# Attention and adapters in one kernel: load tiles of 128 rows by 16 units in place of 256 rows by 8, two parts in place of four, ten adapter chains of four blocks, and a new order

## The chip, the cores and the metric

The kernel runs on one core of a Trainium2 chip. The metric is device time in microseconds (us) of one execution; the time before is the median of three runs. A profile is one further execution, taken by the hardware profiler; its span runs from the first to the last instruction of the core. Engines are named as in the profile: PE (TensorE, matrix multiply) and PEld (its weight loads), DVE (VectorE), ACT (ScalarE), POOL (GpSimd), SP (SyncE, which only issues DMAs). DMAs are issued from SP, ACT and POOL and carried out by 16 DMA engines.

## What is computed

Sliding-window attention (window 32 to both sides) over 8 batches of 8 heads, 576 positions, 64 numbers a head; then a mixture of adapters of rank 16, of which each token takes the best two of eight. Cut to what matters:

```python
batch, n_heads, seq, head_dim = (8, 8, 576, 64)      # q, k, v: float32
scores = scale * np.matmul(q, k.transpose(0, 1, 3, 2))
mask = np.abs(pos[:, None] - pos[None, :]) <= 32
scores = np.where(mask, scores, -1000000000.0)
attn = softmax(scores);  attn_out = np.matmul(attn, v)
x = attn_out.transpose(0, 2, 1, 3).reshape(4608, 512)  # all heads of a token side by side
logits = x @ w_gate                                    # 8 experts
w = softmax of the two largest logits
out = x + sum over the two of w * ((x @ A[e]) @ B[e])  # float32, 4608 x 512
```

## The kernel before

**Units and halves.** A unit is one head of one batch, 576 x 64 numbers. The 128 partitions are two halves of 64: batches 0 to 3 use the lower, batches 4 to 7 the upper (index `g` in the loads), so that one 128-row operation works on a unit of either half. Per half there are 32 units.

**Parts and tiles.** The work has four parts `s` (`SB = 4`), each one batch of either half, 8 units wide. q, k and v come in nine tiles `t`. Tiles `2s` and `2s+1` hold 256 rows of the 8 units of part `s`; query rows begin 32 later than key rows. Tile 8 (`XT`) holds the rest for all 32 units: keys 512 to 575, and for the queries rows 0 to 31 and 544 to 575.

**Loads.** `load_qk` (L305) brings each q or k tile with two DMAs of 512 KB from SP, one for each half, into a buffer `raw` (five of them, 1 MB each); the query tile 8 has four of 256 KB. Each partition gets 16 rows of one unit, 4 KB that lie together in memory; `run_parts` (L288) sets which: with `"h (n r) d -> n h (r d)"` the run of 16 rows, `n`, is the outer index and the head `h` the inner one. For tile 8 it is `"u (n r) d -> u n (r d)"`, the unit outside. A tile is cast to 16 bits in two halves (POOL, ACT or DVE), turned by PE into a PSUM bank (8 matmuls of 128 columns, L335, against `swap`, which also sorts the partitions by head, or `ident`), and copied out to `qT` or `kT` (L352). `load_v` (L371) issues four DMAs of 128 KB for each tile from POOL, which cast on the way; DVE turns them (L388).

**Attention.** `score(s, a)` takes key block `a` (64 keys) of all 8 heads of a part and of both halves: two matmuls put the mask down (L423), 16 multiply keys and queries (L429), ACT takes the exponential (L435). `pv` (L462) multiplies by v for five or six heads of a block `g` of 128 tokens (L475); DVE divides (L487, L494). Block `g` needs key blocks `2g-1` to `2g+1`. So block 0 needs tile 8's queries, and blocks 2 to 4 need the second tile of the part.

**Adapters.** `moe` (L503) is a chain for some blocks of both halves: transposes (L520), a copy out (L182 on ACT, L180 on DVE), the product with gate and A weights (L560), the choice of two experts in eleven small operations on DVE and one on ACT (L570 to L591), the gated product (L601), a transpose (L610), a copy out, the product with B (L634), the sum with x (by PE with a second matmul, L637, and a copy out, L645; or by DVE, L648), and a store of 128 tokens x 512 (SP, L655). Each part has two chains, of four and of six blocks: eight in all.

**Order.** Nothing is scheduled on the chip: the numbers of `ORDER` set the sequence in which all of these operations are handed to their engines, `ON` the engine where two could do it, `HOME` the buffer of a pool. Each engine works through its list strictly in turn. The DMAs that SP and ACT issue take eight semaphores (`DMAHW0` to `DMAHW7`) in turn, so a DMA waits until the eighth before it has landed.

Of the kernel before, what the change touches and what calls it, by code (L numbers as in the profile page):

```python
# [16 lines left out]
D = 64  # L17
NB = 9
NH = 8
SB = 4  # L20
XT = 2 * SB
GS = 172
# [81 lines left out]
def kernel(  # L104
# [14 lines left out]
    POOLS = {"B": 8, "raw": 5, "c16": 6, "v16": 3, "xq": 1,  # L119
             "qT": 2, "kT": 4, "vt": 4, "PT": 7, "xa": 2, "xb": 1, "xT": 1, "zs": 2, "zT": 2, "ob": 4,  # L120
# [4 lines left out]
    def many(name, shape, dt, pool=sb):  # L125
# [7 lines left out]
        "qT": many("qT", [128, NH, NB * 64], F16),  # L133
# [3 lines left out]
        "xa": many("xa", [128, 2, 2 * DD], F16),  # L137
        "xb": many("xb", [128, 2, 3 * DD], F16),
        "xT": many("xT", [128, 6, 4, 128], F16),
        "zs": many("zs", [128, 6, ER], F16),  # L140
        "zT": many("zT", [128, 6, 128], F16),
# [16 lines left out]
    swap = sb.tile([128, 128], F16, name="swap")  # L158
# [120 lines left out]
    grows = {w: x.rearrange("(g b) h n d -> g b h n d", g=2) for w, x in (("q", q), ("k", k), ("v", v))}  # L279
    qT, kT, vt = {}, {}, {}  # L280
    for s in range(SB):
        qT[s] = buf("qT", f"qT{s}")
    xq = buf("xq", "xq")

    def due_of(t):
        return {0: -100, XT: 24}.get(t, 72 * (t // 2) + 32 * (t % 2))

    def run_parts(w, t):  # L288

        r = []  # L290
        for g in range(2):
            x = grows[w][g]
            if t < XT:
                r0 = 256 * (t % 2) + (32 if w == "q" else 0)
                i = x[t // 2, :, r0:r0 + 256].rearrange("h (n r) d -> n h (r d)", r=16)
                r.append((g, 0, 128, i))
                continue
            u = x.rearrange("b h n d -> (b h) n d")
            rows = [(0, 512, 576)] if w == "k" else [(0, 0, 32), (64, 544, 576)]
            for p0, a, b in rows:  # L300
                i = u[:, a:b].rearrange("u (n r) d -> u n (r d)", r=16)
                r.append((g, p0, 2 * (b - a), i))
        return r

    def load_qk(w, t):  # L305
        due = due_of(t) + (32 if (w, t) == ("k", XT) else 0)
# [3 lines left out]
        dst = kT[t] if w == "k" else xq if t == XT else qT[t // 2]  # L310
# [7 lines left out]
        for hf in range(2):  # L318
# [37 lines left out]
    def ends(s):  # L356

        def go(eng):
            w = ap(qT[s]).bitcast(F32)
            o = dataclasses.replace(w, ap=[list(w.ap[0]), [272, 2], [288, NH], [1, 16]])  # L360
            i = ap(xq).bitcast(F32).rearrange("m (e u r) -> m e u r", e=2, r=16)[:, :, NH * s:NH * s + NH]
            (nc.scalar.copy if eng == "ACT" else nc.gpsimd.tensor_copy)(out=o, in_=i)  # L362
        op({"POOL": 0.45, "ACT": act(256)}, 0, go, bufs=[xq, qT[s]], need=[("qT", XT)], make=[("ends", s)],
           prio=due_of(2 * s) + (24 if s == 0 else -10))

    def load_v(t):
        v16, dst = buf("v16", f"v16_{t}"), buf("vt", f"vt{t}")
        vt[t] = dst
        due = 54 if t == XT else due_of(t) if t else -90
        for g in range(2):  # L370
            for f in range(2):  # L371
                p0 = 64 * g + 32 * f
                x = grows["v"][g]
                if t < XT:
                    r0 = 256 * (t % 2)
                    src = x[t // 2, :, r0:r0 + 256].rearrange("h (a f r) d -> f h a (r d)", f=2, r=32)[f]
                else:
                    src = x.rearrange("b h n d -> (b h) n d")[:, 512:576].rearrange(
                        "u (f r) d -> f u (r d)", f=2)[f]
# [15 lines left out]
    for s in range(SB):  # L395
        ends(s)
# [4 lines left out]
    def slot(u, a):  # L401

        s, h = divmod(u, NH)
        return (2 * s + a // 4, 4 * h + a % 4) if a < 8 else (XT, u)

    def score(s, a):

        ti = (s, a)
        ps = buf("B", f"ps{ti}", 2)
        PT[ti] = pt = buf("PT", f"PT{ti}")  # L410
        t = slot(NH * s, a)[0]
        need = {"mask", "ident", ("kT", t)}
        need |= {("qT", 2 * s)} if a < 5 else set()
        need |= {("qT", 2 * s + 1)} if a > 3 else set()
        need |= {("ends", s)} if a in (0, NB - 1) else set()
        lo, hi = max(0, 64 * a - 32), min(576, 64 * a + 96)
        c0 = lo - (64 * a - 32)

        def go():
            p = ap(ps).rearrange("m (i c) -> m i c", c=128)  # L420
            for j in range(2):
                m = slice(64 * j, 64 * j + 64)
                nc.tensor.matmul(out=p[:, 4 * j:4 * j + 4], lhsT=twice[m],  # L423
                                 rhs=bcast(mask[m], 1, 4), start=True, stop=False)
            for h in range(NH):
                sl = slot(NH * s + h, a)[1]
                for g in range(2):
                    m = slice(64 * g, 64 * g + 64)
                    nc.tensor.matmul(out=p[m, h, c0:c0 + hi - lo], lhsT=ap(kT[t])[m, 64 * sl:64 * sl + 64],  # L429
                                     rhs=ap(qT[s])[m, h, lo:hi], start=False, stop=h % 4 == 3)  # L430
        dur = mm(512) + 0.02 + 8 * (mm(hi - lo) + 0.004)
        pr = 72 * s + 8 * a
        op("PE", dur, go, bufs=[ps, kT[t], qT[s]], need=sorted(need, key=str),
           make=[("ps", ti)], prio=pr, mode=1, count=2 + 2 * NH)
# [5 lines left out]
    for s in range(SB):  # L440
        for a in range(NB):
            score(s, a)
# [3 lines left out]
    for s in range(SB):  # L446
        xs[s, 0], xs[s, 1] = buf("xa", f"xa{s}"), buf("xb", f"xb{s}")

    def x_part(s, g):

        return (xs[s, 0], g) if g < 2 else (xs[s, 1], g - 2)

    def pv(s, i0, n):

        items = [(NH * s + i % NH, i // NH) for i in range(i0, i0 + n)]
        token = (s, i0)
        po, rc = buf("B", f"po{token}", 2), buf("rc", f"rc{token}")
        xd, at = x_part(s, items[0][1])
        ops, bufs, need = [], {po}, set()
        for j, (u, g) in enumerate(items):  # L460
            mine = [(a, off) for a, off in ((2 * g - 1, 128), (2 * g, 64), (2 * g + 1, 0))
                    if 0 <= a < NB]  # L462
            for n, (a, off) in enumerate(mine):
                ti, pos = (s, a), u % NH
                t, sl = slot(u, a)
                ops.append((j, ti, pos, off, t, sl, n == 0, n == len(mine) - 1))
                bufs |= {PT[ti], vt[t]}
                need |= {("PT", ti), ("vt", t)}
        last = 9 * s + max(x[1][1] for x in ops)
# [11 lines left out]
        n = len(items)  # L481
# [20 lines left out]

    def moe(s, items, p0, step):  # L503

        xT = buf("xT", f"xT{s}{items[0]}")
        n = len(items)
        tok = (s, items[0])
        xd, first = x_part(s, items[0][1])

        def xp():  # L510

            return ap(xd).rearrange("p b (g c) -> p b g c", c=DD)[:, :, first:]
        for j in range(0, n, 2):
            two = items[j:j + 2]
            tp = buf("B", f"tx{s}{two}")

            def turn(two=two, tp=tp):
                for i, (b, g) in enumerate(two):
                    for c in range(4):
                        nc.tensor.matmul(  # L520
                            out=ap16(tp)[:, 512 * i + 128 * c:512 * i + 128 * c + 128],
                            lhsT=xp()[:, b, g - items[0][1]].rearrange("p (m c) -> p c m", c=4)[:, c],
# [3 lines left out]
               need=[("x", s, g) for _, g in two], make=[("tx", tok, j)], prio=pr, count=4 * len(two))  # L526
# [67 lines left out]
        for w, pz in enumerate(pzs):  # L594
# [25 lines left out]
            for j in range(0, k, 2):  # L620
                pair = [items[i] for i in mine[j:j + 2]]
                m = len(pair)
                pd, ob = buf("B", f"pd{s}{pair}", m), buf("ob", f"ob{s}{pair}")
                pq = pr2 + step * (0.4 + 0.2 * j)
                dt = (s, pair[0])

                def x_of(pair=pair, m=m):
                    return xp()[:, :, pair[0][1] - items[0][1]]
                by_pe = BY_PE(s, w, j)
# [28 lines left out]
    for s in range(SB):  # L658
        moe(s, [(b, g) for g in (0, 1) for b in range(2)], 72 * s + 46, 4)
# [105 lines left out]
```

## Time and profile before

| | |
|---|---|
| time, median of 3 runs | 165.09 us (164.57 to 165.52) |
| the profiled execution's own time, and its span | 166.1 us, 164.3 us |
| busy: PE, DVE, ACT, POOL | 118.9, 92.6, 81.8, 53.6 us |
| mean granted clock of TensorE | 0.873 of full speed |
| read from memory, written | 28.85 MB, 9.44 MB |
| loads of q and k | 34 DMAs of 512 KB and 4 of 256 KB, by SP: 18.87 MB |

The last line counts 18 DMAs for k, and 16 and 4 (of 256 KB) for q. A share is of the span unless it is called a share of the DMA engines: that is the mean over the 16 of them, and 1.00 or a little over it means that none was free. The GB/s beside it count the bytes as written, so that v, which arrives in 32 bits and is written in 16, counts half.

### The profile page before, as it was taken

To read this page: it belongs to the slowest core of one execution; us is meant where nothing else is said; L and a number is where in the kernel's file an instruction comes from. 1 tells how busy PE (TensorE), PEld (TensorE's weight loads), DVE (VectorE), ACT (ScalarE), POOL (GpSimd) and SP (SyncE) were. 2 spreads that over 40 slices of the span, in tenths; PEclk is the share of its full clock that TensorE was granted. 3 is DMA by queue.
4 is the path that set the end of the run, shared out by engine and by line. 5 is a ranking of instruction groups with operands and counts; after the bars stand their busy time and mean duration, and the time that the engine had idled before them with its cause. 6 is when DMAs were issued, how large, how long until landed. Compare 5 with 4: busy or idle time off the path is not lost.

```text
span 164.3 us, 5141 instructions
## 1 busy us (share of the span) xinstructions
PE 118.9 (72%) x2206; PEld 85.8 (52%) x2206; DVE 92.6 (56%) x187; ACT 81.8 (50%) x119; POOL 53.6 (33%) x90
## 2 busy tenths in 40 slices
PE   7804228627980695868989978998999999975740
PEld 3203215325850583658756757665768766765310
DVE  4003445106503554979789957776856768847720
ACT  4002006704392065767298645775688874833340
POOL 8962000054660729604736924208100000000000
PEclk9975555765696599999999999999999999999995
DMA  4999993999999999999999999991040046271285
GB/s 117 243 217 221 217 206 60 260 241 310 240 243 230 234 246 235 238 227 252 284 338 241 341 261 303 358 293 66 0 134 34 4 141 233 93 261 54 89 309 177
DMA packets 14566, 33.90 MB, mean 206 GB/s; under 512 B 4048, under 2 KB 4048, under 8 KB 14544
## 3 DMA queue, kind: packets, MB, share of 16 engines
q1 hardware_dynamic: 10464, 28.32, 61.3%
q0 software_dynamic: 2752, 4.72, 15.4%
q10 hardware_dynamic: 1328, 0.54, 1.9%
q8 instruction: 17, 0.28, 0.7%
q14 instruction: 5, 0.04, 0.1%
HBM read 28.85 MB, written 9.44 MB: 233 GB/s over the span
## 4 chain that ended last, share of the span: by engine, by line
PE 42%; DMA 37%; DVE 10%; issue 4%; ACT 2%; ACTq 1%; SPq 0%; POOL 0%; DVEq 0%; POOLq 0%
DMA raw<-in_q_dram 16%; DMA ob<-in_moe_A_dram 15%; PE banks L429 8%; PE banks L475 6%; DMA v<-in_v_dram 6%; PE banks L335 5%; PE banks L634 5%; PE banks L560 5%; PE banks L423 5%; PE banks L520 4%; PE banks L637 3%; DVE xb L494 3%; DVE xa L494 2%; PE banks L610 1%; ACT PT L435 1%
## 5 line engine op out<-in xcount | busy, mean ns | idle before, releaser
L327 POOL CAST c<-raw 128x1024 f16<-128x1024 f32 x28 | 28.5, 1049 | 51.6 <-DMA raw<-in_q_dram 36.3
L435 ACT ACTIVATE PT<-banks 128x1024 f16<-128x1024 f32 x36 | 36.0, 1028 | 18.5 <-PE banks L429 17.2
L335 PE MATMUL banks<-swap,c 128*128 128x128 f16 x256 | 21.2, 241 | 16.7 <-ACT c L325 6.8
L335 PEld LDWEIGHTS <-c 128*128 128x128 f16 x288 | 19.8, 110 | 23.9 <-ACT c L325 11.9
L429 PE MATMUL banks<-qT,kT 64*64 64x128 f16 (+1 forms) x576 | 23.7, 225 | 0.3 <-ACT qT L362 0.2
L429 PEld LDWEIGHTS <-kT 64*64 64x64 f16 x576 | 17.8, 112 | 10.9 <-issue 10.7
L388 DVE STREAM_TRANSPOSE vt<-v 128x1024 f32<-128x1024 f32 x9 | 18.5, 2055 | 8.5 <-DMA v<-in_v_dram 8.5
L380 POOL DMA_DIRECT2D v<-in_v_dram x36 | 19.5, 555 | 6.5 <-DMA v<-in_v_dram 3.9
L475 PE MATMUL banks<-vt,PT 64*128 64x65 f16 x832 | 18.3, 197 | 1.9 <-issue 1.5
L475 PEld LDWEIGHTS <-PT 64*128 64x128 f16 x832 | 15.8, 99 | 4.8 <-issue 3.2
L494 DVE TENSOR_TENSOR xb<-banks,rc 128x768 f16<-128x768 f32 x16 | 15.1, 956 | 4.9 <-PE banks L520 4.6
L182 ACT COPY xT<-banks 128x512 f32<-128x512 f32 x16 | 9.1, 589 | 15.3 <-PE banks L520 13.0
L634 PE MATMUL banks<-Bw,zT 128*128 128x512 f16 x40 | 14.3, 381 | 2.9 <-ACT zT L182 1.9
L423 PE MATMUL banks<-mask,twice 64*128 64x512 f16 x72 | 15.3, 409 | 1.5 <-DVE xa L494 1.0
L325 ACT CAST c<-raw 128x1024 f16<-128x1024 f32 x5 | 5.2, 1049 | 19.3 <-DMA raw<-in_q_dram 10.1
L645 ACT COPY ob<-banks 128x1024 f32<-128x1024 f32 x11 | 10.9, 1013 | 5.5 <-PE banks L637 5.5
L487 DVE RECIPROCAL rc<-banks 128x12 f32<-128x12 f32 (+1 forms) x28 | 6.2, 223 | 11.0 <-PE banks L475 10.5
L560 PE MATMUL banks<-WA,xT 128*128 128x136 f16 x160 | 11.1, 223 | 1.4 <-issue 1.4
L560 PEld LDWEIGHTS <-xT 128*128 128x128 f16 x160 | 9.8, 98 | 2.2 <-issue 1.7
L494 DVE TENSOR_TENSOR xa<-banks,rc 128x640 f16<-128x640 f32 (+1 forms) x12 | 10.4, 866 | 0.4
L352 ACT COPY kT<-banks 128x512 f32<-128x512 f32 x14 | 7.9, 592 | 4.3 <-PE banks L335 4.2
L327 DVE CAST c<-raw 128x1024 f16<-128x1024 f32 x3 | 2.0, 691 | 13.4 <-DMA raw<-in_k_dram 10.6
(61 smaller groups left out, 129.7 us busy)
## 6 DMA issues: line engine op xcount, KB each, us to landing
raw<-in_k_dram SPq DMA_DIRECT2D x18, 512.0 KB, 13.5
raw<-in_q_dram SPq DMA_DIRECT2D x16, 512.0 KB, 11.4
out_dram<-ob SPq DMA_DIRECT2D x24, 256.0 KB, 3.7
v<-in_v_dram POOLq DMA_DIRECT2D x36, 128.0 KB, 10.6
out_dram<-ob SPq DMA_DIRECT2D x16, 192.0 KB, 2.8
raw<-in_q_dram SPq DMA_DIRECT2D x4, 256.0 KB, 16.2
ob<-in_moe_B_dram ACTq DMA_DIRECT2D x1, 256.0 KB, 5.3
ob<-in_moe_A_dram ACTq DMA_DIRECT2D x1, 256.0 KB, 24.8
```

Of the source, the lines that this page charges most:

```text
L327: (nc.vector if eng == "DVE" else nc.gpsimd).tensor_copy(out=o, in_=i)
L335: nc.tensor.matmul(out=ap16(tp)[:, 128 * r:128 * r + 128], lhsT=ap(c16)[:, r], rhs=swap if t < XT else ident, is_transpose=True, start=Tru ...
L380: op("POOL", 0.5, lambda p0=p0, src=src: nc.gpsimd.dma_start(out=ap(v16)[p0:p0 + 32], in_=src), bufs=[v16], make=[("v", t, "16")], prio=-6 ...
L388: nc.vector.transpose(out=o, in_=i)
L423: nc.tensor.matmul(out=p[:, 4 * j:4 * j + 4], lhsT=twice[m], rhs=bcast(mask[m], 1, 4), start=True, stop=False)
L429: nc.tensor.matmul(out=p[m, h, c0:c0 + hi - lo], lhsT=ap(kT[t])[m, 64 * sl:64 * sl + 64], rhs=ap(qT[s])[m, h, lo:hi], start=False, stop=h ...
L435: op("ACT", act(1024), lambda: nc.scalar.activation(out=ap(pt)[:, :, 64:192].rearrange("m i (x b r) -> m i x b r", b=2, r=16), in_=ap(ps). ...
L475: nc.tensor.matmul(out=ap(po)[:, 512 * g + VD * j:512 * g + VD * j + VD], lhsT=ap(PT[ti])[m, pos, off:off + 128], rhs=ap(vt[t])[m, sl, 0:V ...
L494: nc.vector.tensor_tensor(out=o, in0=i, in1=ap(rc)[:, 0:n].to_broadcast([128, n, 2, D]), op=ALU.mult)
L560: nc.tensor.matmul(out=ap(pz)[:, o:o + ER + E], lhsT=ap(xT)[:, i, c, :], rhs=WA[:, c, :], start=(c == 0), stop=(c == 3))
L634: nc.tensor.matmul(out=o, lhsT=ap(zT)[:, j + i], rhs=Bw, start=True, stop=not by_pe)
L645: (nc.vector.tensor_copy if eng == "DVE" else nc.scalar.copy)(out=ap(ob)[:, 0:m], in_=i0)
```

## The change

A tile now holds 128 rows (two key blocks) of the 16 units of two batches in each half, so the same 512 KB a DMA. There are two parts `p` (`SP = 2`) with four such tiles each, and tile 8 as before. In every q and k load the 16 units are now the outer index and the runs of 16 rows the inner one; in the v loads the 16 units take the place of 8 heads. Tiles thus come out sorted by unit, and `swap` and its making are gone. The query rows of a part lie in two tiles (`qT[p, half]`) of 288 columns; key block 4 straddles them, and its score matmuls are cut in two there. `pv` works on one block at a time (three groups of 6, 5 and 5 heads-and-batches, 30 in place of 28), and each adapter chain takes one block of four batches: ten chains of four. The sum with x is done by PE for 32 of 40 blocks in place of 30. Buffers: `raw` 5 to 4, `qT` 2 to 3 (half as wide in columns, twice in units), `kT` 4 to 3, `PT` 7 to 8, `xT` 1 to 2, three `x` in place of two `xa` and one `xb`. `ORDER`, `ON` and `HOME` are new throughout.

```diff
-SB = 4
-XT = 2 * SB
-GS = 172
+SP = 2
+NU = 16
+XT = 4 * SP
+GS = 256
...
-    POOLS = {"B": 8, "raw": 5, "c16": 6, "v16": 3, "xq": 1,
-             "qT": 2, "kT": 4, "vt": 4, "PT": 7, "xa": 2, "xb": 1, "xT": 1, "zs": 2, "zT": 2, "ob": 4,
+    POOLS = {"B": 8, "raw": 4, "c16": 6, "v16": 3, "xq": 1,
+             "qT": 3, "kT": 3, "vt": 4, "PT": 8, "x": 3, "xT": 2, "zs": 2, "zT": 2, "ob": 4,
...
-    grows = {w: x.rearrange("(g b) h n d -> g b h n d", g=2) for w, x in (("q", q), ("k", k), ("v", v))}
+    urows = {w: x.rearrange("(g b) h n d -> g (b h) n d", g=2) for w, x in (("q", q), ("k", k), ("v", v))}
...
             if t < XT:
-                r0 = 256 * (t % 2) + (32 if w == "q" else 0)
-                i = x[t // 2, :, r0:r0 + 256].rearrange("h (n r) d -> n h (r d)", r=16)
-                r.append((g, 0, 128, i))
-                continue
-            u = x.rearrange("b h n d -> (b h) n d")
-            rows = [(0, 512, 576)] if w == "k" else [(0, 0, 32), (64, 544, 576)]
+                r0 = 128 * (t % 4) + (32 if w == "q" else 0)
+                rows = [(0, r0, r0 + 128)]
+                u = u[NU * (t // 4):NU * (t // 4) + NU]
+            else:
+                rows = [(0, 512, 576)] if w == "k" else [(0, 0, 32), (64, 544, 576)]
             for p0, a, b in rows:
                 i = u[:, a:b].rearrange("u (n r) d -> u n (r d)", r=16)
...
-                                     rhs=swap if t < XT else ident, is_transpose=True,
+                                     rhs=ident, is_transpose=True,
...
-                    src = x[t // 2, :, r0:r0 + 256].rearrange("h (a f r) d -> f h a (r d)", f=2, r=32)[f]
+                    src = x[NU * (t // 4):NU * (t // 4) + NU, r0:r0 + 128].rearrange(
+                        "u (a f r) d -> f u a (r d)", f=2, r=32)[f]
...
+        cuts = [lo, 288, hi] if lo < 288 < hi else [lo, hi]
...
+                for c0, c1 in zip(cuts, cuts[1:]):
+                    hq = c0 // 288
+                    o0 = c0 - (64 * a - 32)
+                    for g in range(2):
+                        m = slice(64 * g, 64 * g + 64)
+                        nc.tensor.matmul(out=ps_[m, h, o0:o0 + c1 - c0],
+                                         lhsT=ap(kT[t])[m, 64 * sl:64 * sl + 64],
+                                         rhs=ap(qT[p, hq])[m, i, c0 - 288 * hq:c1 - 288 * hq], start=False,
+                                         stop=h % 4 == 3 and c1 == hi)
...
-        for i0, n in ((0, 6), (6, 5), (11, 5), (16, 6), (22, 6), (28, 6), (34, 6)):
-            pv(s, i0, n)
+        for g in range(5):
+            for i0, n in ((0, 6), (6, 5), (11, 5)):
+                pv(p, g, i0, n)
...
-        moe(s, [(b, g) for g in (0, 1) for b in range(2)], 72 * s + 46, 4)
-        moe(s, [(b, g) for g in (2, 3, 4) for b in range(2)], 72 * s + 86, 4)
+        for g in range(5):
+            moe(p, g, 144 * p + (32 * g + 46 if g < 4 else 158), 4)
...
-    return s >= 1
+    return p > 0 or g > 1
```

**SP's queue at the start.** Rows are the DMAs that SP issues, with buffer and source; in brackets are the semaphores each waits for. Before:

```order
L313 DMA raw0_61<-in_q_dram 128x1x1024
L313 DMA raw1_62<-in_k_dram 128x1x1024 x2
L313 DMA raw2_63<-in_q_dram 64x1x1024
L313 DMA raw0_61<-in_q_dram 128x1x1024
L313 DMA raw2_63<-in_q_dram 64x1x1024 [waits DMAHW0_49]
L313 DMA raw2_63<-in_q_dram 64x1x1024 [waits DMAHW1_49]
L313 DMA raw2_63<-in_q_dram 64x1x1024 [waits DMAHW2_49]
L313 DMA raw3_64<-in_q_dram 128x1x1024 [waits DMAHW3_49]
```

And after the change:

```order
L305 DMA raw0_61<-in_k_dram 128x1x1024
L305 DMA raw1_62<-in_q_dram 64x1x1024
L305 DMA raw0_61<-in_k_dram 128x1x1024
L305 DMA raw2_63<-in_q_dram 128x1x1024 x2
L305 DMA raw1_62<-in_q_dram 64x1x1024 [waits DMAHW0_49]
L305 DMA raw1_62<-in_q_dram 64x1x1024 [waits DMAHW1_49]
L305 DMA raw1_62<-in_q_dram 64x1x1024 [waits DMAHW2_49]
L305 DMA raw3_64<-in_k_dram 128x1x1024 [waits DMAHW3_49]
```

The rows of 64 partitions are the four pieces of the query tile 8. ACT issues three DMAs beside these: the gate weights, B and A before, B, A and the gate weights now. A's semaphore was `DMAHW3`: the cast that reads A waited for it (L272). So the ninth load, that of tile 1, waited for A, after all four pieces. Now the cast of the gate weights waits for `DMAHW4`, and the other two of ACT's hold `DMAHW0` and `DMAHW2`; A is the later of them, so the fourth piece of tile 8 waits for A, and tile 1 stands behind it.

**POOL's queue at the start**, casts and the DMAs of v, from the end of the mask's making. Before:

```order
L206 COPY mask_115<-mask0_114 128x128
L380 DMA v161_73<-in_v_dram 32x1x2048
L380 DMA v162_74<-in_v_dram 32x1x2048 x2
L380 DMA v161_73<-in_v_dram 32x1x2048
L327 CAST c160_66<-raw3_64 128x1024
```

And after the change:

```order
L197 COPY mask_115<-mask0_114 128x128
masks.py:197 MEMSET ident_112 128x128
masks.py:199 AFFINE_SELECT ident_112<-ident_112 128x128
L371 DMA v160_71<-in_v_dram 32x1x2048 x4
L319 CAST c165_70<-raw1_62 128x1024
L371 DMA v161_72<-in_v_dram 32x1x2048
L371 DMA v162_73<-in_v_dram 32x1x2048 x2
L319 CAST c160_65<-raw3_64 128x1024
```

Before, eleven DMAs of v stood ahead of POOL's first cast. Now four do; the first cast is that of the query tile 8, and the v loads of the next tiles stand behind it.

**ACT's queue at the end**: copies out of PSUM. `xT` and `zT` belong to a chain, `ob` is the output of two blocks, an ACTIVATE of 32 or 48 elements is the exponential of a chain's gate. Before:

```order
L182 COPY xT0_96<-banks_110 128x512
L578 ACTIVATE banks_110<-sm1_106 128x6x8
L182 COPY zT0_99<-banks_110 128x256
L645 COPY ob1_102<-banks_110 128x1024
L182 COPY zT1_100<-banks_110 128x384
L645 COPY ob0_101<-banks_110 128x1024
L645 COPY ob3_104<-banks_110 128x1024
```

And after the change:

```order
L181 COPY xT1_97<-banks_111 128x512 x2
L639 COPY ob0_102<-banks_111 128x1024
L572 ACTIVATE banks_111<-sm1_107 128x4x8
L639 COPY ob1_103<-banks_111 128x1024
L639 COPY ob3_105<-banks_111 128x1024
L639 COPY ob2_104<-banks_111 128x1024
L639 COPY ob0_102<-banks_111 128x1024
```

Before, the last chain gave three outputs, of which ACT copied two and DVE the last. Now the last two chains give two each, all four copied by ACT, and DVE makes their `zT`.

## Rows read from the trace of the kernel before

**Rows 1.** Windows by stage: stretch, length, busy us of engines (count), clock, DMA share, GB/s.

```profile
core 0: us, PE busy (x) PEld busy (x) DVE busy (x) ACT busy (x) POOL busy (x), PEclk, DMA share, GB/s
27.00:65.00 38.00, 24.42 (x434) 18.23 (x432) 14.78 (x28) 15.73 (x26) 17.49 (x24) 0.73 1.01 241
65.00:112.00 47.00, 40.79 (x898) 30.76 (x900) 38.62 (x71) 30.79 (x45) 21.21 (x30) 1.00 1.04 282
112.00:145.00 33.00, 32.34 (x740) 23.71 (x734) 23.30 (x48) 24.06 (x32) 3.64 (x4) 1.00 0.25 86
145.00:164.30 19.30, 9.54 (x92) 5.88 (x90) 8.75 (x25) 5.90 (x10) 0.00 (x0) 0.89 0.53 182
```

**Rows 2.** Chain that ended last, its start: start us, length us, what.

```profile
1.64 24.82 DMA ob<-in_moe_A_dram
...
27.08 6.42 DMA raw<-in_q_dram
```

**Rows 3.** Windows of the loads, columns as in group 1.

```profile
11.00:22.80 11.80, 3.78 (x32) 3.25 (x32) 4.83 (x9) 1.04 (x1) 1.60 (x3) 0.50 1.08 215
...
22.80:27.80 5.00, 2.44 (x18) 1.65 (x18) 1.37 (x2) 3.03 (x5) 0.00 (x0) 0.50 0.54 92
...
27.80:36.60 8.80, 4.38 (x62) 3.09 (x60) 1.52 (x2) 3.17 (x4) 2.38 (x3) 0.69 1.02 239
37.70:39.80 2.10, 1.65 (x22) 1.27 (x21) 2.03 (x2) 1.38 (x3) 0.48 (x1) 0.50 1.00 369
```

**Rows 4.** DMA queues, 0 to 27 us, then 36.6 to 39.8: packets, MB, share.

```profile
q1 hardware_dynamic: 896, 3.15, 51.0%
q0 software_dynamic: 880, 1.44, 29.0%
q10 hardware_dynamic: 1328, 0.54, 11.6%
...
q1 hardware_dynamic: 289, 1.05, 100.3%
```

**Rows 5.** The same on the page, over the whole span.

```profile
q1 hardware_dynamic: 10464, 28.32, 61.3%
q0 software_dynamic: 2752, 4.72, 15.4%
```

**Rows 6.** Chain that ended last: single groups of PE at full clock.

```profile
73.28 0.45 PE banks L335 x8
...
75.31 0.89 PE banks L520 x16
...
83.16 0.56 PE banks L429 x16
...
86.33 0.32 PE banks L423 x2
86.65 0.46 PE banks L429 x16
...
101.64 1.42 PE banks L560 x24
...
126.01 0.22 PE banks L610 x4
...
129.49 0.22 PE banks L634
...
135.29 0.58 PE banks L475 x30
```

**Rows 7.** Chain that ended last, its end.

```profile
143.79 0.62 PE banks L475 x32
...
150.20 0.20 DVE sm L591
...
153.22 0.97 DVE zs L601
...
158.17 1.22 DVE ob L645
```

More of the change, by code (lines that the diff above doesn't have):

```diff
@@ L132 @@
         "xq": many("xq", [128, 2048], F16),
-        "qT": many("qT", [128, NH, NB * 64], F16),
+        "qT": many("qT", [128, NU, NB * 32], F16),
         "kT": many("kT", [128, 2048], F16),
@@ L136 @@
         "PT": many("PT", [128, 8, 256], F16),
[L137 to L141, printed above, removed]
+        "x": many("x", [128, 2, 2 * DD], F16),
+        "xT": many("xT", [128, 4, 4, 128], F16),
+        "zs": many("zs", [128, 4, ER], F16),
+        "zT": many("zT", [128, 4, 128], F16),
         "ob": many("ob", [128, 2, DD], F32),
@@ L309, in load_qk @@
             kT[t] = buf("kT", f"kT{t}")
[L310 removed]
+        dst = kT[t] if w == "k" else xq if t == XT else qT[t // 4, t % 4 // 2]
         raw = buf("raw", f"raw{w}{t}")
@@ L354, in load_qk, with ends @@
                bufs=[tp, dst], need=[(w, t, hf, "T")], make=[(w + "T", t)], prio=pr)
-    def ends(s):
+    def ends(p, e):
         def go(eng):
-            w = ap(qT[s]).bitcast(F32)
-            o = dataclasses.replace(w, ap=[list(w.ap[0]), [272, 2], [288, NH], [1, 16]])
-            i = ap(xq).bitcast(F32).rearrange("m (e u r) -> m e u r", e=2, r=16)[:, :, NH * s:NH * s + NH]
+            o = ap(qT[p, e]).bitcast(F32)[:, :, 128 * e:128 * e + 16]
+            i = ap(xq).bitcast(F32).rearrange("m (e u r) -> m e u r", e=2, r=16)[:, e, NU * p:NU * p + NU]
             (nc.scalar.copy if eng == "ACT" else nc.gpsimd.tensor_copy)(out=o, in_=i)
-        op({"POOL": 0.45, "ACT": act(256)}, 0, go, bufs=[xq, qT[s]], need=[("qT", XT)], make=[("ends", s)],
-           prio=due_of(2 * s) + (24 if s == 0 else -10))
+        op({"POOL": 0.45, "ACT": act(256)}, 0, go, bufs=[xq, qT[p, e]], need=[("qT", XT)],
+           make=[("ends", p, e)], prio=due_of(4 * p) + (24 if p == 0 else -10) + 100 * e)
     def load_v(t):
@@ L368, in load_v @@
         vt[t] = dst
-        due = 54 if t == XT else due_of(t) if t else -90
+        due = 100 if t == XT else due_of(t) if t else -90
         for g in range(2):
@@ L394, with slot, score @@
         load_v(t)
-    for s in range(SB):
-        ends(s)
+    for p in range(SP):
+        for e in range(2):
+            ends(p, e)
     PT = {}
[L401 to L408, printed above, removed]
+    def slot(p, i, a):
+        return (4 * p + a // 2, 2 * i + a % 2) if a < 8 else (XT, NU * p + i)
+    def score(p, a, half):
+        ti = (p, a, half)
         ps = buf("B", f"ps{ti}", 2)
@@ L410, in score @@
         PT[ti] = pt = buf("PT", f"PT{ti}")
-        t = slot(NH * s, a)[0]
+        t = slot(p, 0, a)[0]
         need = {"mask", "ident", ("kT", t)}
-        need |= {("qT", 2 * s)} if a < 5 else set()
-        need |= {("qT", 2 * s + 1)} if a > 3 else set()
-        need |= {("ends", s)} if a in (0, NB - 1) else set()
+        need |= {("qT", 4 * p + j) for j in {max(a - 1, 0) // 2, min(a // 2, 3)}}
+        need |= {("ends", p, 0)} if a == 0 else {("ends", p, 1)} if a == NB - 1 else set()
         lo, hi = max(0, 64 * a - 32), min(576, 64 * a + 96)
-        c0 = lo - (64 * a - 32)
+        cuts = [lo, 288, hi] if lo < 288 < hi else [lo, hi]
@@ L419, in go @@
         def go():
-            p = ap(ps).rearrange("m (i c) -> m i c", c=128)
+            ps_ = ap(ps).rearrange("m (i c) -> m i c", c=128)
             for j in range(2):
                 m = slice(64 * j, 64 * j + 64)
-                nc.tensor.matmul(out=p[:, 4 * j:4 * j + 4], lhsT=twice[m],
+                nc.tensor.matmul(out=ps_[:, 4 * j:4 * j + 4], lhsT=twice[m],
                                  rhs=bcast(mask[m], 1, 4), start=True, stop=False)
[L425 to L434, printed above, removed]
+            for h in range(8):
+                i = 8 * half + h
+                sl = slot(p, i, a)[1]
+                for c0, c1 in zip(cuts, cuts[1:]):
[7 more added lines that the diff above has]
+                                         stop=h % 4 == 3 and c1 == hi)
@@ L435, in score @@
+        n = len(cuts) - 1
+        dur = mm(512) + 0.02 + 8 * (mm(hi - lo) + 0.004 * n)
+        pr = 144 * p + 16 * a + 8 * half
+        op("PE", dur, go, bufs=[ps, kT[t]] + [qT[p, c // 288] for c in cuts[:-1]], need=sorted(need, key=str),
+           make=[("ps", ti)], prio=pr, mode=1, count=2 + 16 * n)
         op("ACT", act(1024), lambda: nc.scalar.activation(
@@ L438, in score, with pv @@
             bufs=[ps, pt], need=[("ps", ti)], make=[("PT", ti)], prio=pr)
-    for s in range(SB):
+    for p in range(SP):
         for a in range(NB):
-            score(s, a)
+            for half in range(2):
+                score(p, a, half)
     xs = {}
[L446 to L456, printed above, removed]
+    for p in range(SP):
+        for g in range(5):
+            xs[p, g] = buf("x", f"x{p}{g}")
+    def pv(p, g, i0, n):
+        token = (p, g, i0)
         po, rc = buf("B", f"po{token}", 2), buf("rc", f"rc{token}")
-        xd, at = x_part(s, items[0][1])
+        xd = xs[p, g]
         ops, bufs, need = [], {po}, set()
[L460 to L466, printed above, removed]
+        mine = [(a, off) for a, off in ((2 * g - 1, 128), (2 * g, 64), (2 * g + 1, 0)) if 0 <= a < NB]
+        for j, i in enumerate(range(i0, i0 + n)):
+            for m, (a, off) in enumerate(mine):
+                ti, pos = (p, a, i // 8), i % 8
+                t, sl = slot(p, i, a)
+                ops.append((j, ti, pos, off, t, sl, m == 0, m == len(mine) - 1))
                 bufs |= {PT[ti], vt[t]}
                 need |= {("PT", ti), ("vt", t)}
-        last = 9 * s + max(x[1][1] for x in ops)
+        last = 18 * p + 2 * mine[-1][0] + (i0 + n - 1) // 8
         def go():
@@ L525, in moe @@
             op("PE", 4 * len(two) * mm(128), turn, bufs=[xd, tp],
-               need=[("x", s, g) for _, g in two], make=[("tx", tok, j)], prio=pr, count=4 * len(two))
+               need=[("x", p, g)], make=[("tx", tok, j)], prio=pr, count=4 * len(two))
             def evict(eng, j=j, m=len(two), tp=tp):
```

95 lines of the change are left out of this document (44 added, 51 removed), and 84 rows, old and new, of tables (HOME, ORDER).

## The prediction

> **What bounds the kernel now.** I read the windows by stage first, because a share over the whole span mixes stages with different limits [rows 1]. From 27 to 65 us the DMA engines have a share of 1.01: none is free, while PE is busy for 24.4 of 38 us at a mean clock of 0.73. From 65 to 145 us PE is busy for 40.79 + 32.34 = 73.1 of 80 us, 91%, at full clock, although the DMA engines stay full to 112. After 145 only the last chain and the stores are left: 19.3 us. So the first 65 us belong to the loads, the next 80 to PE, the rest to a tail.
>
> Then the chain of waits, for what the loads wait for [rows 2]. Its first long piece is not a load of q or k but the adapter weights A, issued at 1.64 us and landed at 26.5. The next is a query tile that SP could only issue then, since it stood behind A's semaphore. The price shows in the window from 22.8 to 27.8 us, where the DMA share falls to 0.54 [rows 3]: 0.46 x 5 = 2.3 us of all engines lost.
>
> Last, the rate of the loads, in the windows and the queues [rows 3, 4]. From 27.8 to 36.6 us four DMAs of tile 1 run at 239 GB/s with every engine busy (1.02). From 36.6 to 39.8 us the queue moves 1.05 MB, two DMAs: by the order of SP's queue they are key tile 8. That is 328 GB/s, and 369 in the undisturbed middle, at a share of 1.00 again. The number of bytes per partition is the same (4 KB) and the engines are equally full; what differs is the pattern. Tile 8 has the unit as outer index, so neighbouring partitions read runs that follow each other in memory; tile 1 has the run outside, so neighbouring partitions read different heads. The change gives every tile tile 8's order.
>
> **The change part by part.** *Loads.* 18.87 MB at 239 GB/s take 79 us of full engines; at 369, 51. v took 15.4% of 164.3 us [rows 5], 25 us, and keeps its bytes. Queue q1 took 61.3%, 101 us, of which 79 were q and k, so the stores took 22. The new total is 51 + 25 + 22 + 3 for ACT's queue (11.6% of 27 us [rows 4]) = 101 us, no longer more than PE needs, and the loads stand ahead of most stores. Between the ends 239 (no gain) and 369 I take 369, the nearest row in pattern and run length.
>
> *The start.* Up to 27 us the engines moved 3.15 MB for SP, eleven v DMAs (29.0%, 7.8 us) and ACT's weights (3.1 us) [rows 4]. Now the first score needs key tile 0, query tile 8 and query tile 0: again 3.15 MB, but only four v DMAs stand ahead, 7.8 x 4/11 = 2.8 us. At 369 GB/s this is 8.5 + 2.8 + 3.1 = 14.4 us, and with 2 us before the first bytes the last piece, which waits for A, lands near 16.5. A cast, a transposition, a copy and a score put the first scores at about 20.5. If the pieces run at 239 GB/s it is 4.7 us later, 25. The v loads moved behind POOL's first cast are those of the next two tiles; they wait some 10 us longer, and need their transposition on DVE only before the first product with v, which follows the first exponentials. If that cover is gone, the first products with v come that much later while scores go on; I price it in the start-up loss below.
>
> *PE's work.* From single groups of the chain at full clock [rows 6]: 36 turned half tiles x 0.45 = 16.2; 36 masks x 0.32 = 11.5; scores 28 x 0.56 + 8 x 0.46 = 19.4; pv 832/30 x 0.58 = 16.1; transposes of x 160/16 x 0.89 = 8.9; gate and A 160/24 x 1.42 = 9.5; transposes of z 40/4 x 0.22 = 2.2; 70 wide products x 0.22 = 15.4. Sum 99.2 us. The change adds two identity products, 0.44, and cuts key block 4's scores: 64 more matmuls, half as wide, in four groups of 16. If a group cost by columns alone this is nothing; if by count alone 4 x 0.56 = 2.2. The 8 edge groups, with fewer columns and as many matmuls, take 0.46, so two halves cost at least about 2 x 0.46 - 0.56 = 0.36 by that row; I take 4 x 0.36 = 1.4. Together 101.0. Without `swap` nothing else changes in the transposes.
>
> *DVE, ACT, POOL.* DVE loses five of nine 1024-wide outputs (5 x 1.22 = 6.1 [rows 7]) and gets two more chains' small operations (2 x 11 x 0.2 = 4.4): about 91 us in place of 92.6. The outputs go to ACT, which gains about as much. Both stay under PE's sum, and POOL's casts and issues keep their number. I cost these at nothing; the cover is PE, and the case without it is the DVE rival.
>
> *The tail.* The last product with v ends at 143.79 + 0.62 = 144.4 [rows 7], 19.9 us before the end. The last chain has four blocks in place of six: a third less of the gated product (0.97/3 = 0.32) and of the gate product (1.42/3 = 0.47 [rows 6]) and one output less, 4 x 0.22 = 0.88, with ACT's copy instead of DVE's 1.22 for the last. I take 1.9 off: 18.0. PE's work in it is 9.54 x 0.89 = 8.5 us at full clock.
>
> *The sum.* Of 101.0 us PE does six half tiles (2.7) before the first score and 8.5 in the tail. The rest, 89.8, at the 91% of the middle stages takes 98.7 us. For a slow start I take 12 us (tiles still short, clock low) at the pace of the stage from 27 to 65, 24.42/38 x 0.73 = 0.47, in place of 0.91: 12 x 0.44 = 5.3 lost. Then 20.5 + 98.7 + 5.3 + 18.0 = 142.5 us of span. The profiled execution's own time is 1.8 us above its span, and 1.0 above the median of the runs shown, so the median stands 0.8 above the span: **143 us**.
>
> Its own range: 98% as from 112 to 145 us, no start loss, tail 17 gives 20.5 + 91.6 + 17 + 0.8 = 130; 85%, a loss over 18 us (7.9), tail 20 gives 155.
>
> **The rivals.** *Loads keep their rate (A).* Against tile 8's 369 GB/s stands query tile 8: also unit outside, though with runs of 8 KB where key tile 8 has 16 and the new tiles 32. Its pieces ran somewhere in 11 to 22.8 us at 215 GB/s and a share of 1.08, beside v and A [rows 3]. If the pattern isn't the cause, the loads stay the bound to about 110 us. Then only the 2.3 us of idle engines and 1.9 of tail can be saved: 165.1 - 4.2 = 161, and with half of the first lost again 162. [...]
>
> *The order on DVE and ACT binds.* DVE is busy 38.62 + 23.30 = 61.9 of 80 us [rows 1], 77%, and each engine works strictly in turn; with 30 pv groups and ten chains there are more handovers. If PE is held to the 65-to-112 pace throughout (40.79/47 = 87%), with a start loss of 8 and an unchanged tail: 20.5 + 103.5 + 8 + 19.9 + 0.8 = 153.
>
> [...]
>
> **How the numbers follow.** Forecast 0.62, A 0.18, DVE 0.10, C 0.10. A difference under 0.5%, 0.8 us, is about what a measurement of this kernel can't tell from none. Forecast and DVE case are faster; A's 162 is faster in most of its spread, and I give it 0.12 faster, 0.05 same, 0.01 slower: faster 0.84, same 0.05, slower 0.11. The range runs from 132, just inside the low end, to 163, with A in it: outside lie C (0.10), some 0.05 of the forecast's low tail and 0.05 of A's upper one.
>
> **What would show it.** Right: the first q and k loads at over 330 GB/s in a window where they are alone; A landed by 17 us and first scores by 21; the DMA share well under 1 before 90 us; PE over 90% busy from about 35 us on; a tail near 18 us. Wrong: windows of loads at 240 GB/s with a share of 1 (A) or under 227 (C); PE waiting for DVE or ACT, not for tiles, in the middle (DVE); v landing so late that PE idles after the first scores.

## The result, and the profile after

The changed kernel takes 158.98 us (median of 4 runs, 154.86 to 162.05) against 164.83 us before: a ratio of 0.946, with an interval of 0.933 to 0.960. Timed once more it took 157.27 us (6 runs, 155.44 to 158.84; ratio 0.948, 0.942 to 0.954). The ratios and their intervals leave out executions more than 1.5% above the kernel's fastest, so that the first is not the quotient of the two medians. So it is faster, by 5% and not by the 13% forecast. The profiled execution took 154.86 us of its own and has a span of 152.8 us, 11.5 less than before, where the medians differ by 6 to 8.

The windows of the profile after, with the columns of [rows 1]:

```profile
22.80:27.80 5.00, 3.97 (x41) 2.85 (x43) 3.11 (x7) 2.51 (x5) 3.77 (x6) 0.54 1.04 256
33.00:51.00 18.00, 12.73 (x292) 10.79 (x293) 8.92 (x18) 8.49 (x15) 8.40 (x13) 0.91 1.04 251
51.20:52.50 1.30, 0.65 (x12) 0.53 (x10) 1.16 (x8) 1.30 (x3) 0.58 (x1) 1.00 1.02 369
76.00:105.00 29.00, 25.59 (x527) 18.31 (x525) 20.64 (x52) 19.98 (x30) 13.62 (x21) 1.00 1.05 276
107.00:136.20 29.20, 28.85 (x733) 21.75 (x731) 21.92 (x58) 22.16 (x31) 2.72 (x3) 1.00 0.30 99
136.20:152.80 16.60, 9.78 (x90) 5.74 (x88) 7.09 (x27) 7.82 (x11) 0.00 (x0) 0.92 0.61 217
```

The gap of [rows 3] at 22.8 us is gone: a share of 1.04 in place of 0.54. But the loads run at 250 GB/s with every engine busy, hardly more than the 239 before, and the last of them land near 106 us. Key tile 8, at 51 us, again goes at 369. So tile 8's rate was real and the new tiles, whose unit is outside as tile 8's is, don't have it. The queue of q, k and the stores moved the same 28.32 MB in as much engine time: 66.1% of 152.8 us is 101.0 us, against 61.3% of 164.3 us, 100.7, before [rows 5].

```profile
q1 hardware_dynamic: 10464, 28.32, 66.1%
```

PE has 88% of the window from 76 us on and 99% only from 107, when the loads are over.

The chain of waits says the same (start, length, what; first its shares by engine, then long pieces of its first half, then its end):

```profile
DMA 47%; PE 33%; DVE 5%; issue 3%; ACT 3%; POOL 3%; SPq 2%; POOLq 0%; ACTq 0%
```
```profile
2.74 12.42 DMA raw<-in_q_dram
15.18 15.93 DMA raw<-in_q_dram
...
33.90 17.87 DMA raw<-in_q_dram
...
54.55 18.06 DMA raw<-in_q_dram
...
135.50 0.71 PE banks L468 x40
...
143.72 0.70 DVE zs L595
...
147.37 1.02 ACT ob L639
```

A is no longer in it: it landed 7.6 us after its issue, in place of 24.8 [rows 2].

```profile
DMA to landing us min/median/max: 7.6/7.6/7.6
```

In its stead stand four pieces of loads of q. The last product with v ends at 136.2 us and the tail behind it is 16.6 us long, against 19.9 [rows 7].

The first scores, after and then before (count; ns; first and last start):

```profile
L423 PE MATMUL banks<-qT,kT x640: 192/216/313, 26.1 to 133.1; 64*64 64x128 f16 x96, 64*64 64x96 f16 x32, 64*64 64x64 f16 x32
```
```profile
L429 PE MATMUL banks<-qT,kT x576: 202/216/313, 27.8 to 141.9; 64*64 64x128 f16 x150, 64*64 64x96 f16 x42
```

The scores start at 26.1 us, 1.7 earlier than before; 20.5 was forecast.

### The profile page after: what moved, and what is told of

It is laid out like the page before. It is cut to its first block, busy times and chain, and to the rows that moved or that the text cites. A ratio compares the mean times of both kernels' runs of the same rounds, so it can differ in the third digit from the quotient of the medians.

```text
span 152.8 us, 5311 instructions
## 1 busy us (share of the span) xinstructions
PE 118.0 (77%) x2272; PEld 85.0 (56%) x2272; DVE 90.6 (59%) x214; ACT 85.1 (56%) x122; POOL 51.7 (34%) x88
## 3 DMA queue, kind: packets, MB, share of 16 engines
q1 hardware_dynamic: 10464, 28.32, 66.1%
## 4 chain that ended last, share of the span: by engine, by line
DMA 47%; PE 33%; DVE 5%; issue 3%; ACT 3%; POOL 3%; SPq 2%; POOLq 0%; ACTq 0%
DMA raw<-in_q_dram 42%; PE banks L423 6%; DMA v<-in_v_dram 5%; PE banks L468 5%; PE banks L554 4%; PE banks L514 4%; PE banks L628 4%; PE banks L631 3%; PE banks L327 3%; PE banks L413 3%; POOL c L319 2%; SPq L305 2%; DVE vt L379 1%; ACT ob L639 1%; DVE x L485 1%
## 5 line engine op out<-in xcount | busy, mean ns | idle before, releaser
L432 ACT ACTIVATE PT<-banks 128x1024 f16<-128x1024 f32 x36 | 35.3, 1025 | 10.1 <-PE banks L423 7.0
L327 PE MATMUL banks<-ident,c 128*128 128x128 f16 x288 | 23.6, 237 | 17.8 <-ACT c L317 8.9
L485 DVE TENSOR_TENSOR x<-banks,rc 128x640 f16<-128x640 f32 (+1 forms) x30 | 25.5, 862 | 0.7
L423 PE MATMUL banks<-qT,kT 64*64 64x128 f16 (+2 forms) x640 | 23.7, 218 | 0.6 <-ACT qT L344 0.4
L371 POOL DMA_DIRECT2D v<-in_v_dram x36 | 18.0, 514 | 8.6 <-DVE rc L479 5.5
L639 ACT COPY ob<-banks 128x1024 f32<-128x1024 f32 x16 | 15.7, 1015 | 5.3 <-PE banks L631 4.2
L181 ACT COPY xT<-banks 128x512 f32<-128x512 f32 x19 | 10.8, 591 | 3.4 <-PE banks L514 3.2
L479 DVE RECIPROCAL rc<-banks 128x10 f32<-128x10 f32 (+1 forms) x30 | 6.3, 215 | 10.2 <-PE banks L468 8.2
L631 PE MATMUL banks<-x,ident 128*128 128x512 f16 x32 | 12.1, 379 | 0.0
L514 PE MATMUL banks<-ident,x 128*128 128x128 f16 x160 | 11.8, 221 | 0.4 <-DVE x L485 0.4
```

The lines of the kernel that those rows point to most:

```text
L371: op("POOL", 0.5, lambda p0=p0, src=src: nc.gpsimd.dma_start(out=ap(v16)[p0:p0 + 32], in_=src), bufs=[v16], make=[("v", t, "16")], prio=-6 ...
L423: nc.tensor.matmul(out=ps_[m, h, o0:o0 + c1 - c0], lhsT=ap(kT[t])[m, 64 * sl:64 * sl + 64], rhs=ap(qT[p, hq])[m, i, c0 - 288 * hq:c1 - 288 ...
L432: op("ACT", act(1024), lambda: nc.scalar.activation(out=ap(pt)[:, :, 64:192].rearrange("m i (x b r) -> m i x b r", b=2, r=16), in_=ap(ps). ...
L514: nc.tensor.matmul(out=ap16(tp)[:, 512 * i + 128 * c:512 * i + 128 * c + 128], lhsT=xp()[:, ab, bl].rearrange("p (m c) -> p c m", c=4)[:, ...
```

## The experiments

**Which pattern is fast.** The first kernel does nothing but load, one pattern a stage:

```python
def runs_outside(x, g, j):                    # stages 2 and 10: 256 rows of 8 heads
    ...rearrange("h (n r) d -> n h (r d)", r=16)
def units_outside(x, g, j, rows):             # 1, 3, 8: 128 rows; 4, 9: 64; 6: 256; 7: 512
    ...rearrange("u (n r) d -> u n (r d)", r=16)
def last_rows(x, g, j):                       # stage 5: unit(x, g)[:, 512:576]
...
for j in range(4):
    for g in range(2):
        nc.sync.dma_start(out=raw[:, 2 * j + g], in_=src(g, j))
```

> The kernel only loads: ten stages in turn, each of eight DMAs of 512 KB from SP with a wait for all of them behind it, nothing else running; it computes nothing and its output is zeros. Stages: 1 and 3 runs of 128 rows of 16 units, unit outside (the changed kernel's), 2 256 rows of 8 heads, run outside (the kernel before's), 4 64 rows of 32 units from the first rows on, 5 the last 64 rows of 32 units (key tile 8), 6 256 rows of 8 units, 7 512 rows of 4 units, all unit outside; 8 to 10 as 1, 4 and 2 but from q in place of k. Theory 1, it is how many units a DMA spans: stages 4, 5 and 9 run near 370 GB/s, 1 and 3 near 250, 2 near 240. Theory 2, it is where tile 8 lies, at the end of each unit: only stage 5 is fast. Theory 3, it was what ran beside tile 8: all stages are alike.

Windows inside stages 1, 2 and 4 to 10 (length; DVE and POOL busy; clock; DMA share; GB/s):

```profile
2.00:21.00 19.00, 0.99 (x1) 0.00 (x0) 1.00 1.01 240
24.00:42.00 18.00, 0.00 (x0) 0.00 (x0) 1.00 0.97 223
...
65.00:77.50 12.50, 0.00 (x0) 0.00 (x0) 1.00 0.87 330
80.00:91.20 11.20, 0.00 (x0) 0.00 (x0) 1.00 0.95 367
95.00:115.00 20.00, 0.00 (x0) 0.00 (x0) 1.00 0.51 181
125.00:160.00 35.00, 0.00 (x0) 0.00 (x0) 1.00 0.26 105
166.00:182.50 16.50, 0.00 (x0) 0.00 (x0) 1.00 0.98 228
186.00:197.00 11.00, 0.00 (x0) 0.00 (x0) 1.00 0.93 355
200.00:217.00 17.00, 0.00 (x0) 0.00 (x0) 1.00 1.01 235
```

Theory 1 stands: 64 rows of 32 units are fast wherever they lie (330 and 367; from q 355), 128 rows of 16 units run at 240, hardly over the pattern before (223), and from q the two are alike (228 and 235). With 8 or 4 units outside the share of the engines falls to 0.51 and 0.26, and the rate to 181 and 105. From 16 to 32 units the share doesn't rise (1.01 in stage 1, 0.87 and 0.95 in 4 and 5), and yet the rate goes from 240 to 330 and 367.

**The order of the loads, undone.**

```diff
-                r0 = 128 * (t % 4) + (32 if w == "q" else 0)
-                rows = [(0, r0, r0 + 128)]
-                u = u[NU * (t // 4):NU * (t // 4) + NU]
+                r0 = 256 * (t % 2) + (32 if w == "q" else 0)
+                u = u[8 * (t // 2):8 * (t // 2) + 8, r0:r0 + 256]
+                r.append((g, 0, 128, u.rearrange("h (n r) d -> n h (r d)", r=16)))
+                continue
```

> The changed kernel with the loads' order undone: each q and k tile but tile 8 is loaded as before the change, 256 rows of 8 heads with the run outside; nothing else differs, so the attention is computed on the wrong rows. If the new order of the loads gives what the windows of the two profiles show, 250 in place of 239 GB/s while the loads are the bound, the loads end some 3 us later and the time is 2 to 4 us above the changed kernel's. If the order of the loads is worth nothing, the time is the changed kernel's within 1 us.

It takes 157.82 us (157.27 to 159.04; ratio to the kernel before 0.956, 0.949 to 0.962), inside the changed kernel's own spread:

> The changed kernel itself once more, to place its time beside the run with the loads' order undone (157.8 us). If the order of the loads is worth nothing, its median lies between 156 and 160; if it is worth the 2 to 4 us that the windows suggest, between 153.5 and 156.

As told above, 157.27 us. The windows around the end of the loads, of the changed kernel and then of this one:

```profile
105.00:115.00 10.00, 9.65 (x264) 8.10 (x264) 8.70 (x21) 7.59 (x12) 3.02 (x3) 1.00 0.31 114
```
```profile
105.00:115.00 10.00, 10.00 (x265) 8.36 (x262) 8.53 (x16) 7.05 (x10) 3.01 (x3) 1.00 0.31 113
```

The loads end at the same time. The new order of the loads, on which the forecast rested, is worth nothing that stands out of the spread, at most a microsecond or so.

**The rest of the sum, with the loads out of the way.**

```diff
+            def issue(g=g, p0=p0, np_=np_, src=src):
+                if g == 0 or raw.idx not in filled or (w, t) == ("q", XT):
+                    nc.sync.dma_start(out=ap(raw)[p0:p0 + np_, g], in_=src)
+                if g == 1:
+                    filled.add(raw.idx)
```

> The changed kernel without the loads of the upper half (batches 4 to 7) for 14 of its 18 q and k tiles: those work on what an earlier tile left in the buffer, so the output is wrong there; every other instruction stays. 7.3 of 18.9 MB less, at 245 GB/s 30 us less of full engines, about what 369 GB/s would have given. If only the rate of the loads was mis-sized in the prediction, the time comes down to 140 to 147 us. If the order on DVE and ACT binds PE next, it stays above 150.

It takes 144.51 us (142.52 to 145.22; ratio 0.868, 0.858 to 0.878). Two windows of its middle:

```profile
45.00:95.00 50.00, 46.76 (x999) 34.86 (x997) 40.29 (x91) 35.48 (x54) 27.64 (x40) 1.00 0.83 205
95.00:128.00 33.00, 32.65 (x787) 24.99 (x785) 25.70 (x63) 25.07 (x35) 1.04 (x1) 1.00 0.28 94
```

PE is busy for 94% and 99%. The sum of PE's work was right, and neither DVE nor ACT holds it to the 87% of the rival on their order: that rival falls.

**Where the gain came from: A.** Only the order table of the kernel before changes; on ACT's queue it moves one row:

```diff
+L263 DMA ob0_101<-in_moe_A_dram 128x8x64
 L266 DMA wgf_116<-in_moe_w_gate_dram 128x32
 L268 DMA ob0_101<-in_moe_B_dram 128x512
-L263 DMA ob0_101<-in_moe_A_dram 128x8x64
```

> The kernel before with one step moved: the DMA of A is the first that ACT issues, ahead of the gate weights and B. If A's late landing is what opens the gap in the loads, A lands by 12 us, the share of the DMA engines stays at 1 from 22 to 28 us, and the time is 2 to 5 us less. If the loads only run out of buffers somewhere later, the time is the same within 1 us.

It takes 160.92 us (159.68 to 163.55; ratio 0.971, 0.963 to 0.979), 4.7 less. From its trace: A's landing, the window of the gap, and the one in which the loads end:

```profile
DMA to landing us min/median/max: 3.7/3.7/3.7
```
```profile
22.80:27.80 5.00, 2.43 (x18) 1.65 (x18) 1.36 (x2) 3.02 (x5) 0.00 (x0) 0.50 1.05 245
...
105.00:115.00 10.00, 9.59 (x169) 6.44 (x169) 7.37 (x15) 7.47 (x10) 3.99 (x4) 1.00 0.14 50
```

The gap closes and the loads are over by 107 us, as in the changed kernel. That is most of the gain, without any of the rest of the change. It is twice the 2.3 us of idle engines that the forecast counted; what the other half is the runs don't settle.

**Where the gain came from: the last chain.** In the same kernel the last chain does four blocks:

```diff
+        short = s == SB - 1 and n == 6
+        n = 4 if short else n
+        at = {0: 0, 4: 2} if short else {j: j for j in range(0, n, 2)}
```

(its transposes, copies, products, sums and stores run for the pairs in `at` alone).

> The run with A first, and in it the last adapter chain cut from six blocks to four by leaving out the adapters, the sum and the store of one block of two batches (those rows of the output are not written). If the longer chain is what makes the tail of 19.9 us, the tail falls to 16.5 to 17.5 us and the time to 157 to 158.5, that of the changed kernel. If the third pair only fills waits, the tail loses less than 1 us.

It takes 157.24 us (155.93 to 158.71; ratio 0.947, 0.941 to 0.954): 3.7 less than with six, and the changed kernel's time. Its last product with v:

```profile
138.90 0.63 PE banks L475 x32
```

The span is 156.8 us, so the tail is 17.3 us long, 2.6 less than before, as was expected. Not all of the 3.7 us is tail: the two blocks left out are 2 of 40 in the adapters' 36.0 us of PE [rows 6], 1.8 us, which the changed kernel does earlier. So A and the shorter last chain account for the gain within a microsecond or two, and for the tiles, the parts and the load order together nothing is left that can be told from none.

**Why 16 outer steps are slow and 32 are not.** Two more kernels load and do nothing else. Theory P in what follows is a guess of mine, that the writing on chip sets the rate: which partitions are written at one time, and how many bytes.

```python
def runs_32(o, g, j):    # stage 2: 32 runs outside, 4 heads inside
    ...[4 * j:4 * j + 4, 0:512].rearrange("h (n r) d -> n h (r d)", r=16)
def halves(o, g, j):     # stages 6 and 7: two DMAs of 64 partitions
    s = rows(g, j, 128).rearrange("u (m n) x -> m u n x", m=2)
    return [(o[64 * m:64 * m + 64], s[m]) for m in range(2)]
```

> Only loads again, eight times 512 KB of k a stage, a wait for all behind each stage, no computation, output zeros. Stages: 1 the changed kernel's tile (16 units of 8 runs), 2 32 runs of 4 heads with the run outside, 3 64 units of 2 runs, 4 512 KB that lie together, 5 as 1 but every second DMA from ACT's queue, 6 the tile as two DMAs of 64 partitions (16 units of 4 runs each), all from SP, 7 the same with the upper 64 partitions from ACT. [...] Theory H, it is the distance in memory between units: stage 2 is slow like the 256 rows of 8 heads, 6 and 7 are like 1, only 4 is fast.

Windows inside stages 2, 4, 5, 6 and 7:

```profile
22.00:34.00 12.00, 0.00 (x0) 0.00 (x0) 1.00 0.96 354
...
50.00:61.00 11.00, 0.00 (x0) 0.00 (x0) 1.00 0.95 377
63.00:81.00 18.00, 0.00 (x0) 0.00 (x0) 1.00 0.95 233
83.00:101.00 18.00, 0.00 (x0) 0.00 (x0) 1.00 0.96 233
103.00:119.00 16.00, 0.00 (x0) 0.00 (x0) 1.00 0.98 260
```

Theory H falls on stage 2: the run outside, as before the change, but 32 of them, at 354 GB/s. Theory P gets no support from stage 7: the two halves of the partitions from two queues bring 260, not clearly more than the 233 from one. The next kernel keeps the source and moves the destination:

```python
few([...], 16, 1)     # units to partitions b, b+1, b+2, ...: 16 of them
few([...], 16, 8)     # b, b+8, ...
few([...], 16, 4)     # b, b+4, ... inside one half
few([...], 32, 4)     # 32 units: b, b+4, ...
few([...], 32, 1)     # b, b+1, ...
tiles(nc.sync, raw, acc); tiles(nc.gpsimd, raw, acc)
tiles(nc.gpsimd, half, acc16)     # half: 16 bits
```

> Only loads of k again, 4.2 MB a stage, a wait for all behind each, no computation, output zeros. The first five stages read long runs (16 or 8 KB a partition) and differ in the partitions that one DMA writes: 1 16 units to 16 neighbouring partitions, 2 16 units to every eighth partition, 3 16 units to every fourth of one half, 4 32 units to every fourth of all 128, 5 32 units to 32 neighbouring ones. Stages 6 to 8 load the changed kernel's tile: from SP, from POOL, and from POOL cast to 16 bits on the way. [...] Theory D (what is slow is an outer index of 16 as such): stages 1 to 3 are alike at 240, 4 and 5 alike at 350 or more, 8 as 7.

Windows inside stages 1 to 5, 7 and 8 (GB/s as written: stage 8 reads twice that):

```profile
13.00:46.00 33.00, 0.00 (x0) 0.00 (x0) 1.00 0.97 120
49.00:69.00 20.00, 0.00 (x0) 0.00 (x0) 1.00 0.98 208
71.00:88.50 17.50, 0.00 (x0) 0.00 (x0) 1.00 0.96 240
91.00:103.00 12.00, 0.00 (x0) 0.00 (x0) 1.00 0.92 342
106.00:124.50 18.50, 0.00 (x0) 0.00 (x0) 1.00 0.99 216
...
148.00:166.00 18.00, 0.00 (x0) 3.06 (x6) 1.00 0.98 233
169.00:180.00 11.00, 0.00 (x0) 2.73 (x6) 1.00 1.04 188
```

Stages 4 and 5 read the same 32 units; only the partitions differ: 342 against 216 GB/s. Theory D, which made them alike, falls; theory P allows the difference, though I had put stage 4 at 350 or more. And the tile with 16 outer steps, at 233 GB/s from POOL in 32 bits, reads 376 GB/s when it writes 16 bits. So reading this pattern at 233 is not the limit. Stages 1 to 3 read the same rows in the same order too, at 120, 208 and 240 GB/s, and in all five the share of the engines is 0.92 to 0.99: within each of the two groups what differs is the partitions written. That the tile with 16 outer steps is slow for this reason is inferred and not shown.

**A version that follows from it.** The changed kernel with its q and k loads cast on the way; in the order table the loads of the first three tiles stand first on POOL:

```diff
-        "raw": many("raw", [128, 2, 16 * D], F32),
+        "raw": many("raw", [128, 2, 16 * D], F16),
...
-            op("SP", 0.46, lambda g=g, p0=p0, np_=np_, src=src: nc.sync.dma_start(
+            op("POOL", 0.46, lambda g=g, p0=p0, np_=np_, src=src: nc.gpsimd.dma_start(
```

> The changed kernel with its q and k loads issued by POOL, which casts them to 16 bits on the way as v's are, into a buffer half as large; the casts by POOL, ACT and DVE stay as 16-bit copies, and the loads of the first three tiles stand at the front of POOL's list. Theory P: half the bytes are written, the loads run as fast as those with fewer bytes, and the time falls to 143 to 150 us unless POOL's list (36 casts, 36 v loads and now 38 loads more) becomes the bound. Theory D: the loads' rate stays, and the time stays at 155 or above.

It takes 143.77 us (143.07 to 144.41; ratio to the kernel before 0.870, 0.863 to 0.876), the fastest of all. Its first scores, its chain by engine, and two windows:

```profile
L423 PE MATMUL banks<-qT,kT x640: 192/216/240, 17.8 to 121.4; 64*64 64x128 f16 x96, 64*64 64x96 f16 x32, 64*64 64x64 f16 x32
```
```profile
PE 45%; POOL 16%; DMA 13%; DVE 8%; ACT 8%; issue 7%; POOLq 0%; ACTq 0%; DVEq 0%
```
```profile
45.00:90.00 45.00, 38.92 (x794) 28.64 (x790) 33.36 (x68) 30.21 (x45) 32.20 (x50) 0.96 0.99 209
90.00:124.00 34.00, 33.65 (x838) 25.54 (x836) 25.70 (x63) 25.77 (x36) 1.04 (x1) 1.00 0.29 98
```

Scores start at 17.8 us and the loads are over by 90. DMA falls from 47% of the chain to 13%, PE rises from 33% to 45%. The queue that now brings q, k and v:

```profile
q0 software_dynamic: 6944, 14.16, 56.1%
```

That is 79 us of 141.4. Less the 25 of v [rows 5], q and k take some 54 us of full engines, where the prediction counted 79 before the change. The copies in place of the casts are no cheaper on POOL (1.06 us each, 1.05 before). No run tells how much of the earlier start is due to the first loads' place in POOL's list.

## Why the prediction was wrong

**The step that failed** is the rate of the loads: "Between the ends 239 (no gain) and 369 I take 369, the nearest row in pattern and run length." The new tiles ran at 251 GB/s, and with the old pattern the time is the same. I had taken the order of the indices for what set key tile 8 apart. In the load kernels' tiles of 128 partitions the rate went with the number of outer steps: those of 16 went at 223 to 245, those of 32 at 330 to 367, and at 354 with the run outside. With the number goes how many neighbouring partitions belong to one step, 4 in place of 8. At 251 GB/s q and k take 75 us of full engines and not 51, so the loads, not PE, bound the kernel to some 106 us. A row that spoke against 369 was there: query tile 8, unit outside and 215 GB/s [rows 3]. It is no clean case, for it too has 32 steps, but its DMAs write 64 partitions each and ran beside v and A. I used it for the rivals and gave them 0.28 together.

**Rival A happened**, nearly at its time (162 forecast, 157 to 159 measured). The share of the engines could not show it: the loads had 1.02 before and 1.04 after. In the first load kernel it falls only at 8 and 4 outer steps, to 0.51 and 0.26. Between 16 and 32 steps, with 1.01 and 0.95, the difference of 240 to 367 GB/s does not show in it.

**The start** was mis-sized with the rate: first scores at 26.1 us, by the forecast's own lower rate 25. A landed early, as said: by 9 us, where the sign was 17. By the queues' window no v was moved in the kernel's first 10 us.

**The gap at A** I priced at 2.3 us; moving A alone was worth 4.7. **The tail** I took 1.9 off, and 3.3 went. Both terms were right in direction and too small; at their measured size rival A's sum gives 165.1 - 8.0 = 157.1.

**PE's work and pace** were right in sum: with fewer loads 144.5 us, with cast loads 143.8, against a forecast of 143. That they meet so closely is in part luck. With fewer loads the first scores and the last product with v were:

```profile
L429 PE MATMUL banks<-qT,kT x640: 192/216/313, 24.4 to 123.0; 64*64 64x128 f16 x96, 64*64 64x96 f16 x32, 64*64 64x64 f16 x32
```
```profile
125.39 0.71 PE banks L474 x40
```

So scores began 3.9 us later than forecast, the stretch up to 126.1 us took 101.7 in place of 104.0, and the tail to 142.9 was 16.8 in place of 18.0. The pace behind 45 us was 94 to 99% with fewer loads, above the 91% assumed. **DVE and ACT** stayed under PE, as I said. **Rival C**, that loads with the unit outside are the slower ones, below 227 GB/s, had 0.10; what should have slowed them was my guess, and no run shows it. It fell: the new tiles ran at 251, and alone at 240 against 223 with the run outside.

## What to carry to other kernels

A share of 1.00 of the DMA engines does not say that the transfer runs as fast as it can: here it was 1.01 at 240 GB/s and 0.95 at 367. Compare its GB/s with the fastest DMA in the same trace, and before you credit a pattern for the difference, time that pattern alone, since two tiles that look alike can differ in the one number that counts. When loads bound a kernel, try what halves the bytes written on chip before what reorders them: here the changed kernel took 143.8 us with cast loads and 157.3 without, and the new order of its loads gave nothing that stands out of the spread. And look for small DMAs on whose semaphore a big one waits: one row moved on ACT's queue was worth 4.7 us, most of this whole change.

## What the runs showed of the hardware

With the same rows read, the rate of a load differed with the partitions that one DMA writes. With 16 long runs to 16 neighbouring partitions it was 120 GB/s, to every eighth partition 208, to every fourth of one half 240; with 32 runs to every fourth partition 342, to 32 neighbouring ones 216. What on the chip sets these rates is not shown. Nor is it why a tile of 16 steps of 8 partitions went at 223 to 245 GB/s and one of 32 steps of 4 at 330 to 367: no record tells which engine writes which partition, and the two halves of the partitions from two queues brought only 260.

A cast load read 376 GB/s in the pattern that an uncast one read at 233, from the same queue.
